# Sums that read a PSUM bank, one bank in the other pool, and moved Sinkhorn steps in a kernel of fifteen-product groups

## The chip, the cores and the metric

The kernel runs on one core of a Trainium2 chip. The metric is the device time of one execution in microseconds (us). Engines are named as in the profile: PE (TensorE; PEld are its weight loads), DVE (VectorE), ACT (ScalarE), POOL (GpSimd), SP (the queue that issues the DMAs).

## The reference

Three parts follow each other: attention of pooled queries, a feed-forward block (here called mish), and a block of eight experts whose outputs are mixed with weights from a Sinkhorn iteration. The change touches the third alone:

```python
def _moe2_ref(x, w_gate, w1, w2):        # x 1152x512, w1 8x512x1024, w2 8x1024x512
    logits = x @ w_gate
    P = np.exp(logits - logits.max())
    for _ in range(8):
        P /= P.sum(1, keepdims=True) + 1e-09
        P /= P.sum(0, keepdims=True) + 1e-09
        P *= N / E
    out = np.zeros((N, D), dtype=np.float32)
    for e in range(E):
        h = np.maximum(x @ w1[e], 0.0)
        out += P[:, e:e + 1] * (h @ w2[e])
    return out
```

## The kernel before, in words

All engines run queues that the program writes in order (a manual schedule); semaphores hold an instruction back until what it reads or overwrites is ready. Attention, the mish block and the first 512 hidden columns of expert 0 come first and aren't touched. Every float32 matmul is made of three matmuls of halves ("h" for the leading bits of a value, "l" for the rest): weights l by data h, h by l, h by h.

**Groups.** The other 60 chunks of 128 hidden columns (4 to 63) are taken in 20 groups of three. A group's hidden layer is a product of a 3x2 block matrix (three chunks, two halves of the 512 inputs) and a 2x3 block matrix (two halves, three stretches of 384 tokens); instead of 18 block products it makes 15, of sums of blocks that were formed beforehand, and then adds and subtracts the products. `ORDER3` is the order of the products: 9, 13, 3, 11, 12, 1, 2, 5, 10, 14, 7, 8, 0, 6, 4. `product` (L973) issues the six matmuls of one, 128x128 by 128x384, into a PSUM bank. `HOME` says which: bank "ft" collects hidden chunk f of the group and token stretch t. Three banks get one product (01, 10, 22); in the other six a second product is added later (00: 13 then 2, 12: 11 then 8, 11: 12 then 5, 02: 10 then 6, 20: 14 then 0, 21: 7 then 4). The first of the two is needed elsewhere, so `after` (L1024) has it read out between the two.

**Pools.** A bank is asked for when its first product is issued (L978). Banks 01, 10 and 22 come from the pool `ps_o` (three banks), the others from `ps_h` (five); the down projection and the matmuls of the Sinkhorn steps use `ps_o` too. A pool hands out the bank that was released longest ago.

**After a product.** `copy` (L1000) has ACT copy a bank into a temporary in SBUF. `pair` (L1004) has DVE add or subtract two temporaries. `fin` (L1013) finishes a block: DVE adds a temporary to the bank in place (L1016), ACT writes the Relu as the leading half `hhall` (L1020), and DVE writes the rest `hlall` (L1021). This last one is put off until the next `fin` has issued its own DVE addition. After each of the first seven products ACT and POOL split the weights of the product eight places later (L74, L81).

**Down projection.** After the products `down` (L1126) takes nine tiles of 128 tokens in the order 0, 1, 2, 6, 7, 8, 3, 4, 5: nine matmuls each, 128x128 by 128x512 (L1145), three for every hidden chunk, and DVE adds the scaled bank to the output (L1153). Between the tiles `next_weights` forms the weight sums of the next group.

**Sinkhorn.** `gate_step` takes the next of ten small steps: the maximum over partitions, its broadcast and the exponential, and eight iterations (`sinkhorn_cols`, L815), each of one small matmul on PE (L817) and a chain of up to six small DVE instructions (L818 to L812), the last of which writes what the next step's matmul reads. The places of the ten steps are written out by hand: in the loop of the last hidden columns of expert 0 (L1108), in the down projection of that part, in the products of groups 0 and 1 (L1197) and in the down projection of group 0 (L1205).

Of the kernel before, what the change touches and what calls it, by code (L numbers as in the profile page):

```python
# [23 lines left out]
def pool_attention_mish_sinkhorn_kernel(  # L24
# [12 lines left out]
    nc = tc.nc  # L37
# [248 lines left out]
    with ExitStack() as actx:  # L286
# [356 lines left out]
        for g in range(T0 + EARLY):  # L643
# [41 lines left out]
            if g == NQ - 1:  # L685
                sctx.close()
                ps_o = ctx.enter_context(tc.tile_pool(name="ps_o", bufs=3, space=PSUM, side="right"))
# [18 lines left out]
    def hidden(c, a, b):  # L706
        return tuple((y if c == NFC - 1 else x[:, c, :])[:, a:b] for x, y in hall)

    ps_h = ctx.enter_context(tc.tile_pool(name="ps_h", bufs=5, space=PSUM))
# [40 lines left out]
    k = EARLY - 1  # L750
# [82 lines left out]
    def expert_up(i, th, c):  # L833
        nonlocal tick
        ps = ps_h.tile([P, 512], F32, tag="h", name=f"ph{i}_{th}_{c}")
        gemm1(ps, i, c, th, x2h, x2l)
        relu_split(hidden(c, th * TH, (th + 1) * TH), ps[:, 0:TH])
        tick += 1
        run_all(tick)
# [35 lines left out]
    def xblock(x, d, t):  # L875
        return x[:, d * HD:(d + 1) * HD, t * TH:(t + 1) * TH]
# [4 lines left out]
    PLUS = {"+": ALU.add, "-": ALU.subtract}  # L881
# [3 lines left out]
    def x_prep(k):  # L885
        n, a, op, b = XSUM[k]
        get = lambda z: xblock(acc, *z) if isinstance(z, tuple) else xsum[z]
        x = xsum[n] = xt_p.tile([P, HD, TH], F32, tag="xt", name=f"xt{n}")
        nc.vector.tensor_tensor(out=x, in0=get(a), in1=get(b), op=PLUS[op])
        x_flush()  # L890
        if k < len(XSUM) - 2:
            Xb[n] = tuple(tsum.tile([P, HD, TH], F32R, name=f"x{n}{y}") for y in "hl")
            x_split(k)

    def x_split(k):
        n = XSUM[k][0]
        split_hi(nc.scalar, Xb[n][0], xsum[n])
        x_lo.append((nc.gpsimd if k % 2 else nc.vector, Xb[n][1], xsum[n], Xb[n][0]))

    def x_flush():  # L900
        while x_lo:
            split_lo(*x_lo.pop(0))
# [27 lines left out]
    def down_split(g, j):  # L930

        if "all" not in wdt:
            wdt["all"] = tuple(wpools["d0"].tile([P, 4, GF], F32R, tag="wd" + x, name=f"wdb{x}") for x in "hl")
        wh, wl = wdt[g, j] = tuple(y[:, (CH * g + j) % 4, :] for y in wdt["all"])
        split_hi(nc.gpsimd, wh, raws_d[g][j])
        split_lo(nc.gpsimd, wl, raws_d[g][j], wh)
# [20 lines left out]
    def w_split(g, k):  # L957
        n = ORDER3[k]
        x = w_get(g, PLAIN[n]) if n in PLAIN else ws[g, n]
        at_ = (NP * g + k) % NSL  # L960
        dst = tuple(y[:, at_, :, :] for y in wslots)
        split_hi(nc.scalar, dst[0], x)
        split_lo(nc.gpsimd, dst[1], x, dst[0])
        Wb[g, n] = dst
# [7 lines left out]
    cb, tmp = {}, {}  # L972
    los = []  # L973

    def product(g, n):
        c = HOME[n]
        if FIRST[n]:
            pl, tag = (ps_o, "o") if c in ("01", "10", "22") else (ps_h, "h")  # L978
            cb[c] = pl.tile([P, 512], F32, tag=tag, name=f"c{c}_{g}")[:, 0:TH]
        (wh, wl), (xh_, xl_) = Wb[g, n], Xb[n]  # L980
        ops = []
        for d in range(HD):
            ops += [(wl[:, d, :], xh_[:, d, :]), (wh[:, d, :], xl_[:, d, :]), (wh[:, d, :], xh_[:, d, :])]
        for m, (a_, b_) in enumerate(ops):
            nc.tensor.matmul(  # L985
                cb[c], lhsT=a_, rhs=b_, start=FIRST[n] and m == 0, stop=LAST[n] and m == len(ops) - 1,
                skip_group_check=True)
# [5 lines left out]
    def temp(g, x):  # L993
        if x in SPARE:
            i = SPARE.index(x)
            tmp[x] = spare[i % 2][:, i // 2, :]
        else:
            tmp[x] = up_t.tile([P, TH], F32, tag=x, name=f"{x}_{g}")

    def copy(g, x, c):  # L1000
        temp(g, x)
        nc.scalar.activation(tmp[x], cb[c], AF.Copy)  # L1002

    def pair(g, eng, out, a, op, b):  # L1004
        if out not in tmp or out == "s11":
            temp(g, out)
        eng.tensor_tensor(out=tmp[out], in0=tmp[a], in1=tmp[b], op=PLUS[op])  # L1007

    def flush_lo():
        while los:  # L1010
            los.pop(0)()

    def fin(g, c, op, x):  # L1013

        b = cb[c]
        nc.vector.tensor_tensor(out=b, in0=b, in1=tmp[x], op=PLUS[op])  # L1016
        flush_lo()
        f, t = int(c[0]), int(c[1])
        hi, lo = hidden(f, t * TH, (t + 1) * TH)
        nc.scalar.activation(hi, b, AF.Relu)  # L1020
        los.append(lambda: nc.vector.scalar_tensor_tensor(  # L1021
            out=lo, in0=b, scalar=0.0, in1=hi.bitcast(F32), op0=ALU.max, op1=ALU.subtract))

    def after(g, n):  # L1024

        v = nc.vector
        if n == 9:
            copy(g, "t9", "01")
        if n == 13:
            copy(g, "t13", "00")  # L1030
            fin(g, "01", "+", "t13")
        if n == 3:
            copy(g, "t3", "10")
            pair(g, v, "s11", "t3", "-", "t9")
        if n == 11:
            copy(g, "t11", "12")
            fin(g, "10", "+", "t11")
        if n == 12:
            copy(g, "u12", "11")
            pair(g, v, "u12", "u12", "-", "t11")  # L1040
        if n == 1:
            copy(g, "t1", "22")
            pair(g, v, "t13", "t1", "+", "t13")
        if n == 2:
            fin(g, "00", "+", "u12")
        if n == 5:
            fin(g, "11", "+", "s11")
        if n == 10:
            copy(g, "t10", "02")
            fin(g, "22", "-", "t10")  # L1050
            pair(g, v, "t3", "t3", "-", "t10")
        if n == 14:
            copy(g, "u14", "20")
            pair(g, v, "u14", "t1", "-", "u14")
        if n == 7:
            copy(g, "u7", "21")
            pair(g, v, "u7", "u7", "+", "t9")
        if n == 8:
            fin(g, "12", "+", "u14")
        if n == 0:  # L1060
            fin(g, "20", "+", "t3")
        if n == 6:
            fin(g, "02", "-", "u7")
        if n == 4:
            fin(g, "21", "-", "t13")
            flush_lo()
# [28 lines left out]
    def gate_step():  # L1095
        if gate_steps:
            gate_steps.pop(0)()
# [7 lines left out]
    with tc.tile_pool(name="xt", bufs=3, side="right") as xt_p:  # L1105
        todo_x = list(range(len(XSUM)))
        for j, u in enumerate(ups):
            if j in (2, 4):  # L1108
                gate_step()
            expert_up(NG1, *u)  # L1110
            for _ in range(2 if j % 2 else 1):
                if todo_x:
                    x_prep(todo_x.pop(0))
        assert not todo_x
        for n, d, t in ((9, 0, 1), (10, 1, 2), (11, 0, 0), (13, 1, 1)):
            Xb[n] = tuple(xblock(x, d, t) for x in (x2h, x2l))
        for k, d, t in ((-2, 0, 2), (-1, 1, 0)):
            Xb[XSUM[k][0]] = tuple(xblock(x, d, t) for x in (x2h, x2l))
            x_split(len(XSUM) + k)
        x_flush()  # L1120
# [56 lines left out]
    def scale(k):  # L1177
        nc.gpsimd.tensor_scalar(
            oacc[:, TILES[k], :], oacc[:, TILES[k], :], Pm[:, TILES[k], 0:1], 0.0, op0=ALU.mult, op1=ALU.add)
# [9 lines left out]
    for g in range(NG):  # L1189
        for k, n in enumerate(ORDER3):  # L1190
            product(g, n)
            after(g, n)
            if k + NSL < NP:
                w_split(g, k + NSL)
            if k in ((0, 7, 9) if g == 0 else (7, 9)):
                down_split(g, {0: 0, 7: 1, 9: 2}[k])
            if k == 9 and g + 1 < NG:  # L1197
                raw_up(g + 1)
            if (g, k) in ((0, 3), (0, 5), (1, 3)):
                gate_step()  # L1200
            if g == 1 and k in (10, 12, 14):
                assert not gate_steps
                scale(k // 2 - 5)
        for k, t in enumerate(TILES):
            down(g, t)  # L1205
            next_weights(g + 1, k)
            if g == 0 and k in (1, 3, 5):
                gate_step()
            if g == 1 and k + 3 < NTT:
                scale(k + 3)  # L1210
# [30 lines left out]
```

## Time and profile before

| | us |
|---|---|
| median of 3 runs | 1261.66 |
| lowest, highest | 1261.29, 1261.70 |
| profiled execution | 1261.36 |
| its span, first to last instruction | 1259.6 |

The profile is that of one execution. Times in it count from the span's start. The page gives the busy time of every engine; the views asked of the trace give groups of instructions by line with their mean duration, waits with what ended them, the chain that ended last (each step followed back to what released it), and the timeline of one engine. Names like `c` are banks of products, `po` banks of the down projection, `t`, `spareh` and `sparel` the temporaries (u12, t10 and u7 lie in `spareh`, t1, u14 and s11 in `sparel`). A matmul's row is longer than the step from one matmul to the next. The granted TensorE clock was 1.0 of full speed in the whole span.

### The profile page before, as it was taken

To read this page: it belongs to the slowest core of one execution; us is meant where nothing else is said; L and a number is where in the kernel's file an instruction comes from. 1 tells how busy PE (TensorE), PEld (TensorE's weight loads), DVE (VectorE), ACT (ScalarE), POOL (GpSimd) and SP (SyncE) were. 2 spreads that over 40 slices of the span, in tenths; PEclk is the share of its full clock that TensorE was granted. 3 is DMA by queue.
4 is the path that set the end of the run, shared out by engine and by line. 5 is a ranking of instruction groups with operands and counts; after the bars stand their busy time and mean duration, and the time that the engine had idled before them with its cause. 6 is when DMAs were issued, how large, how long until landed. Compare 5 with 4: busy or idle time off the path is not lost.

```text
span 1259.6 us, 19402 instructions
## 1 busy us (share of the span) xinstructions
PE 1230.0 (98%) x6832; PEld 1120.1 (89%) x6832; DVE 921.0 (73%) x1706; ACT 622.0 (49%) x1432; POOL 727.3 (58%) x758
## 2 busy tenths in 40 slices
PE   8999999999999999999999999999999999999998
PEld 7999999999999999878888888888888888888887
DVE  7899999975444335797866779877867778866875
ACT  7899999876554433534333333443333334433331
POOL 7888888644434332556656555655555566556552
PEclk9999999999999999999999999999999999999999
DMA  3333333213222110011110111111101111111111
GB/s 114 97 97 91 89 94 96 76 35 118 84 84 85 52 41 17 9 43 50 51 51 28 37 45 48 46 50 51 51 22 39 51 51 42 52 51 39 33 38 75
DMA packets 55760, 73.15 MB, mean 58 GB/s; under 512 B 5744, under 2 KB 37872, under 8 KB 55664
## 3 DMA queue, kind: packets, MB, share of 16 engines
q1 hardware_dynamic: 55664, 71.93, 19.6%
q8 instruction: 54, 0.88, 0.3%
q14 instruction: 42, 0.34, 0.1%
HBM read 64.50 MB, written 2.36 MB: 53 GB/s over the span
## 4 chain that ended last, share of the span: by engine, by line
PE 31%; DVE 13%; issue 6%; ACT 5%
PE po L1145 27%; DVE c L1016 6%; PE c L985 4%; DVE hlall L1021 3%; DVE t L1007 2%; DVE sparel L1007 2%; ACT hhall L1020 1%; ACT t L1002 1%; ACT spareh L1002 1%; ACT wslotsh L74 1%; DVE s L951 0%; DVE spareh L1007 0%; DVE oacc L1151 0%; DVE Pm L810 0%; DVE Pm L819 0%
## 5 line engine op out<-in xcount | busy, mean ns | idle before, releaser
L81 POOL TENSOR_TENSOR wslotsl<-s,wslotsh 128x256 fp32r<-128x256 f32 x180 | 143.4, 806 | 221.2 <-ACT wslotsh L74 221.1
L1153 DVE SCALAR_TENSOR_TENSOR oacc<-po,Pm,oacc 128x512 f32<-128x512 f32 (+1 forms) x217 | 160.7, 744 | 83.8 <-PE po L1145 79.2
L1145 PE MATMUL po<-wdbh,hlall 128*128 128x512 f32 (+1 forms) x543 | 216.2, 398 | 5.7 <-DVE hlall L1021 5.7
L1145 PE MATMUL po<-wdbl,hhall 128*128 128x512 f32 (+1 forms) x543 | 215.7, 397 | 2.9 <-ACT hhall L1020 0.8
L1145 PE MATMUL po<-wdbh,hhall 128*128 128x512 f32 (+1 forms) x543 | 214.0, 394 | 0.0
L1020 ACT ACTIVATE hhall<-c 128x384 fp32r<-128x384 f32 x180 | 88.5, 492 | 161.1 <-DVE c L1016 158.6
L1002 ACT ACTIVATE t<-c 128x384 f32<-128x384 f32 x80 | 39.1, 489 | 224.8 <-PE c L985 224.8
L81 POOL TENSOR_TENSOR wslotsl<-rawu,wslotsh 128x256 fp32r<-128x256 f32 x120 | 97.0, 822 | 68.6 <-ACT wslotsh L74 68.6
L1145 PEld LDWEIGHTS po<-wdbh,hlall 128*128 128x128 f32 x543 | 102.0, 188 | 34.5 <-DVE hlall L1021 12.0
L1145 PEld LDWEIGHTS po<-wdbl,hhall 128*128 128x128 f32 x543 | 102.0, 188 | 33.4 <-issue 10.5
L1145 PEld LDWEIGHTS po<-wdbh,hhall 128*128 128x128 f32 x543 | 102.0, 188 | 23.4
L501 DVE TENSOR_TENSOR etl<-psT,eth 128x384 fp32r<-128x384 f32 (+1 forms) x240 | 112.1, 504 | 9.4 <-ACT eth L498 9.3
L466 POOL TENSOR_SCALAR e<-e,rc 128x1152 f32<-128x1152 f32 x72 | 89.0, 1236 | 43.7 <-DVE rc L465 16.7
L446 DVE TENSOR_SCALAR_CACHE_REDUCE sc<-psS 128x1152 f32<-128x1152 f32 x72 | 97.4, 1353 | 14.5 <-PE psS L441 13.5
L1021 DVE SCALAR_TENSOR_TENSOR hlall<-c,hhall 128x384 fp32r<-128x384 f32 x180 | 97.8, 543 | 2.0
L498 ACT ACTIVATE eth<-psT 128x384 fp32r<-128x384 f32 (+1 forms) x240 | 92.7, 483 | 8.9 <-PE psT L495 8.8
L985 PE MATMUL c<-x2h,wslotsl 128*128 128x384 f32 x280 | 94.4, 337 | 0.0
L985 PE MATMUL c<-x2h,wslotsh 128*128 128x384 f32 x280 | 94.3, 337 | 0.0
L985 PE MATMUL c<-x2l,wslotsh 128*128 128x384 f32 x280 | 94.0, 336 | 0.0
L454 ACT ACTIVATE e<-sc,nm 128x1152 f32<-128x1152 f32 x72 | 92.1, 1279 | 0.5 <-DVE sc L446 0.5
L495 PE MATMUL psT<-ident,e 128*128 128x128 f32 x648 | 85.5, 275 | 1.3 <-POOL e L466 0.8
L166 POOL TENSOR_TENSOR wt<-wt,raw 128x512 int32<-128x512 int32 x32 | 42.1, 1317 | 75.6 <-DVE wt L160 71.0
(349 smaller groups left out, 3302.2 us busy)
## 6 DMA issues: line engine op xcount, KB each, us to landing
rawd<-in_moe_w_dram SPq DMA_DIRECT2D x60, 256.0 KB, 2.6
rawu<-in_moe_w_dram SPq DMA_DIRECT2D x30, 384.0 KB, 3.2
raw<-in_moe_w_in_dram SPq DMA_DIRECT2D x16, 512.0 KB, 3.9
raw<-in_moe_w_out_dram SPq DMA_DIRECT2D x16, 512.0 KB, 3.6
kraw<-in_k_dram SPq DMA_DIRECT2D x16, 288.0 KB, 3.1
vraw<-in_v_dram SPq DMA_DIRECT2D x16, 288.0 KB, 2.8
qraw<-in_q_dram SPq DMA_DIRECT2D x7, 576.0 KB, 4.3
qT<-qT SPq DMA_DIRECT2D x28, 128.0 KB, 2.5
```

The lines of the kernel that those rows point to most:

```text
L81: eng.tensor_tensor(out=lo, in0=src, in1=hi.bitcast(F32), op=ALU.subtract)
L446: nc.vector.tensor_scalar(sc, ps[:, :, 0:TH], -1.0, None, op0=ALU.mult, op1=ALU.min, accum_out=nm)
L454: nc.scalar.activation(e, sc.rearrange("p a b -> p (a b)"), AF.Exp, bias=nm, scale=-1.0, accum_out=rs)
L466: nc.gpsimd.tensor_scalar(e, e, rc, 0.0, op0=ALU.mult, op1=ALU.add)
L495: nc.tensor.transpose(ps[:, i, :], e[:, c * P:(c + 1) * P], ident)
L498: nc.scalar.activation(eh[:, cs, o:o + b - a], ps[:, 0:3, a:b], AF.Copy)
L501: nc.vector.tensor_tensor(out=el[:, cs, o:o + b - a], in0=ps[:, 0:3, a:b], in1=eh[:, cs, o:o + b - a].bitcast(F32), op=ALU.subtract)
L985: nc.tensor.matmul(cb[c], lhsT=a_, rhs=b_, start=FIRST[n] and m == 0, stop=LAST[n] and m == len(ops) - 1, skip_group_check=True)
L1020: nc.scalar.activation(hi, b, AF.Relu)
L1021: los.append(lambda: nc.vector.scalar_tensor_tensor(out=lo, in0=b, scalar=0.0, in1=hi.bitcast(F32), op0=ALU.max, op1=ALU.subtract))
L1145: nc.tensor.matmul(ps[:, 0:w], lhsT=a, rhs=b[:, cs], start=(n == 0), stop=(n == len(ops) - 1))
L1153: nc.vector.scalar_tensor_tensor(out=oa, in0=ps[:, 0:w], scalar=gate, in1=oa, op0=ALU.mult, op1=ALU.add)
```

## The change

Six calls of `pair` now read one operand from the bank itself (written "@", with the block's name). The copies of u12, u14 and u7 on ACT are gone; those of t3, t1 and t10 stay, since the temporaries are read again later. All six sums stay on DVE, and the sum into t3 now stands ahead of the final addition of block 22 instead of behind its two DVE instructions. Bank 21 is asked from `ps_o`. The ten Sinkhorn steps are the same ones, at other places.

```diff
--- before.py
+++ after.py
@@ -975,7 +975,7 @@
     def product(g, n):
         c = HOME[n]
         if FIRST[n]:
-            pl, tag = (ps_o, "o") if c in ("01", "10", "22") else (ps_h, "h")
+            pl, tag = (ps_o, "o") if c in ("01", "10", "22", "21") else (ps_h, "h")
             cb[c] = pl.tile([P, 512], F32, tag=tag, name=f"c{c}_{g}")[:, 0:TH]
         (wh, wl), (xh_, xl_) = Wb[g, n], Xb[n]
         ops = []
@@ -1001,10 +1001,12 @@
         temp(g, x)
         nc.scalar.activation(tmp[x], cb[c], AF.Copy)
 
-    def pair(g, eng, out, a, op, b):
-        if out not in tmp or out == "s11":
+    def pair(g, out, a, op, b):
+
+        a, b = (cb[x[1:]] if x[0] == "@" else tmp[x] for x in (a, b))
+        if out not in ("t13", "t3"):
             temp(g, out)
-        eng.tensor_tensor(out=tmp[out], in0=tmp[a], in1=tmp[b], op=PLUS[op])
+        nc.vector.tensor_tensor(out=tmp[out], in0=a, in1=b, op=PLUS[op])
 
     def flush_lo():
         while los:
@@ -1023,7 +1025,6 @@
 
     def after(g, n):
 
-        v = nc.vector
         if n == 9:
             copy(g, "t9", "01")
         if n == 13:
@@ -1031,30 +1032,27 @@
             fin(g, "01", "+", "t13")
         if n == 3:
             copy(g, "t3", "10")
-            pair(g, v, "s11", "t3", "-", "t9")
+            pair(g, "s11", "@10", "-", "t9")
         if n == 11:
             copy(g, "t11", "12")
             fin(g, "10", "+", "t11")
         if n == 12:
-            copy(g, "u12", "11")
-            pair(g, v, "u12", "u12", "-", "t11")
+            pair(g, "u12", "@11", "-", "t11")
         if n == 1:
             copy(g, "t1", "22")
-            pair(g, v, "t13", "t1", "+", "t13")
+            pair(g, "t13", "@22", "+", "t13")
         if n == 2:
             fin(g, "00", "+", "u12")
         if n == 5:
             fin(g, "11", "+", "s11")
         if n == 10:
             copy(g, "t10", "02")
+            pair(g, "t3", "t3", "-", "@02")
             fin(g, "22", "-", "t10")
-            pair(g, v, "t3", "t3", "-", "t10")
         if n == 14:
-            copy(g, "u14", "20")
-            pair(g, v, "u14", "t1", "-", "u14")
+            pair(g, "u14", "t1", "-", "@20")
         if n == 7:
-            copy(g, "u7", "21")
-            pair(g, v, "u7", "u7", "+", "t9")
+            pair(g, "u7", "@21", "+", "t9")
         if n == 8:
             fin(g, "12", "+", "u14")
         if n == 0:
@@ -1105,7 +1103,7 @@
     with tc.tile_pool(name="xt", bufs=3, side="right") as xt_p:
         todo_x = list(range(len(XSUM)))
         for j, u in enumerate(ups):
-            if j in (2, 4):
+            if j in (2, 5):
                 gate_step()
             expert_up(NG1, *u)
             for _ in range(2 if j % 2 else 1):
@@ -1196,7 +1194,7 @@
                 down_split(g, {0: 0, 7: 1, 9: 2}[k])
             if k == 9 and g + 1 < NG:
                 raw_up(g + 1)
-            if (g, k) in ((0, 3), (0, 5), (1, 3)):
+            if (g, k) in ((0, 3), (1, 0), (1, 4)):
                 gate_step()
             if g == 1 and k in (10, 12, 14):
                 assert not gate_steps
@@ -1204,7 +1202,7 @@
         for k, t in enumerate(TILES):
             down(g, t)
             next_weights(g + 1, k)
-            if g == 0 and k in (1, 3, 5):
+            if g == 0 and k in (1, 4, 7):
                 gate_step()
             if g == 1 and k + 3 < NTT:
                 scale(k + 3)
```

On DVE, twelve rows in the middle of the products of group 10, before (block names follow the c; the last number is a buffer's; the brackets name the engines whose semaphores an instruction waits for, Activation being ACT):

```order
L1021 SCALAR_TENSOR_TENSOR hlall_4458<-c01_10_9926,hhall_4456 128x384
L1007 TENSOR_TENSOR spareh_6717<-spareh_6717,t11_10_9969 128x384 [waits Activation_49]
L1007 TENSOR_TENSOR t13_10_9944<-sparel_6718,t13_10_9944 128x384 [waits DVE_49,Activation_49]
L1016 TENSOR_TENSOR c00_10_9937<-c00_10_9937,spareh_6717 128x384 [waits DVE_49,PE_49]
L1021 SCALAR_TENSOR_TENSOR hlall_4458<-c10_10_9950,hhall_4456 128x384
L1016 TENSOR_TENSOR c11_10_9976<-c11_10_9976,sparel_6718 128x384 [waits PE_49]
L1021 SCALAR_TENSOR_TENSOR hlall_4458<-c00_10_9937,hhall_4456 128x384 [waits Activation_49]
L1016 TENSOR_TENSOR c22_10_9987<-c22_10_9987,spareh_6717 128x384 [waits Activation_49]
L1021 SCALAR_TENSOR_TENSOR hlall_4458<-c11_10_9976,hhall_4456 128x384
L1007 TENSOR_TENSOR t3_10_9957<-t3_10_9957,spareh_6717 128x384
L1007 TENSOR_TENSOR sparel_6718<-sparel_6718 128x384 [waits Activation_49]
L1007 TENSOR_TENSOR spareh_6717<-spareh_6717,t9_10_9933 128x384 [waits Activation_49]
```

and with the change, where a line number is two higher from `fin` on:

```order
L1023 SCALAR_TENSOR_TENSOR hlall_4458<-c01_10_9896,hhall_4456 128x384
L1009 TENSOR_TENSOR spareh_6717<-c11_10_9946,t11_10_9939 128x384 [waits PE_49]
L1009 TENSOR_TENSOR t13_10_9914<-c22_10_9956,t13_10_9914 128x384 [waits DVE_49,Activation_49]
L1018 TENSOR_TENSOR c00_10_9907<-c00_10_9907,spareh_6717 128x384 [waits DVE_49,PE_49]
L1023 SCALAR_TENSOR_TENSOR hlall_4458<-c10_10_9920,hhall_4456 128x384
L1018 TENSOR_TENSOR c11_10_9946<-c11_10_9946,sparel_6718 128x384 [waits PE_49]
L1023 SCALAR_TENSOR_TENSOR hlall_4458<-c00_10_9907,hhall_4456 128x384 [waits Activation_49]
L1009 TENSOR_TENSOR t3_10_9927<-t3_10_9927,c02_10_9989 128x384 [waits Activation_49]
L1018 TENSOR_TENSOR c22_10_9956<-c22_10_9956,spareh_6717 128x384
L1023 SCALAR_TENSOR_TENSOR hlall_4458<-c11_10_9946,hhall_4456 128x384
L1009 TENSOR_TENSOR sparel_6718<-sparel_6718,c20_10_10001 128x384 [waits PE_49]
L1009 TENSOR_TENSOR spareh_6717<-c21_10_10015,t9_10_9903 128x384 [waits PE_49]
```

The sums (L1007, now L1009) read a bank `c` in place of a copy in `spareh` or `sparel`. Those of u12 (from c11), u14 (from c20) and u7 (from c21) now wait for PE alone; those into t13 and t3 still wait for ACT. The sum into t3 moved ahead of the final addition to c22.

On PE, the first matmul of products 5, 14, 7, 0 and 4 of group 10, before:

```order
L985 MATMUL c11_10_9976<-x5h_6399,wslotsl_6533 128x384 [waits Activation_49,Pool_49]
L985 MATMUL c20_10_10032<-x14h_6426,wslotsl_6533 128x384 [waits DVE_49,Pool_49]
L985 MATMUL c21_10_10047<-x7h_6476,wslotsl_6533 128x384 [waits DVE_49,Pool_49]
L985 MATMUL c20_10_10032<-x2h_6011,wslotsl_6533 128x384 [waits Activation_49,Pool_49]
L985 MATMUL c21_10_10047<-x4h_6482,wslotsl_6533 128x384 [waits Activation_49,Pool_49]
```

and with the change:

```order
L985 MATMUL c11_10_9946<-x5h_6399,wslotsl_6533 128x384 [waits DVE_49,Pool_49]
L985 MATMUL c20_10_10001<-x14h_6426,wslotsl_6533 128x384 [waits Pool_49]
L985 MATMUL c21_10_10015<-x7h_6476,wslotsl_6533 128x384 [waits Pool_49]
L985 MATMUL c20_10_10001<-x2h_6011,wslotsl_6533 128x384 [waits DVE_49,Pool_49]
L985 MATMUL c21_10_10015<-x4h_6482,wslotsl_6533 128x384 [waits DVE_49,Pool_49]
```

Products 5, 0 and 4 add to a bank whose first content ACT had read and DVE reads now. Products 14 and 7 start new banks; neither waits for DVE any more.

## Rows read from the trace of the kernel before

**Rows 1.** The page: busy us, share of the span, instructions of PE.

```profile
PE 1230.0 (98%) x6832; PEld 1120.1 (89%) x6832; DVE 921.0 (73%) x1706; ACT 622.0 (49%) x1432; POOL 727.3 (58%) x758
```

**Rows 2.** Waits of PE: us in total, times, longest us.

```profile
PE c L985 <- DVE hlall L1021: 6.2, 19, 0.3
PE po L1145 <- DVE hlall L1021: 5.7, 19, 0.3
```

**Rows 3.** Chain that ended last, group 10: start us, us, what.

```profile
894.89 2.10 PE c L985 x12
...
904.18 0.46 DVE hlall L1021
...
913.50 17.53 PE po L1145 x74
...
931.04 2.10 PE c L985 x12
```

**Rows 4.** Timeline of PE in group 10: start us, us, instruction, idle before it.

```profile
905.03 0.34 PE L985 MATMUL c<-x14h,wslotsh 128*128 128x384 f32 x1
905.72 0.42 PE L985 MATMUL c<-x7h,wslotsl 128*128 128x384 f32 x1 [0.34 <-DVE hlall L1021]
905.97 0.34 PE L985 MATMUL c<-x7l,wslotsh 128*128 128x384 f32 x1
906.15 0.34 PE L985 MATMUL c<-x7h,wslotsh 128*128 128x384 f32 x1
...
912.21 0.40 PE L1145 MATMUL po<-wdbh,hhall 128*128 128x512 f32 x1
912.73 0.47 PE L1145 MATMUL po<-wdbl,hhall 128*128 128x512 f32 x1
913.50 0.50 PE L1145 MATMUL po<-wdbh,hlall 128*128 128x512 f32 x1 [0.30 <-DVE hlall L1021]
913.84 0.40 PE L1145 MATMUL po<-wdbh,hhall 128*128 128x512 f32 x1
```

**Rows 5.** DVE's groups of L1007: busy us, mean ns, idle us before them.

```profile
L1007 DVE TENSOR_TENSOR spareh<-spareh,t 128x384 f32<-128x384 f32 x40 | 49.3, 1232 | 14.6 <-ACT spareh L1002 14.6
L1007 DVE TENSOR_TENSOR t<-t,spareh 128x384 f32<-128x384 f32 x20 | 24.2, 1210 | 0.0
L1007 DVE TENSOR_TENSOR t<-sparel,t 128x384 f32<-128x384 f32 x20 | 20.8, 1041 | 0.4 <-ACT sparel L1002 0.4
L1007 DVE TENSOR_TENSOR sparel<-sparel 128x384 f32<-128x384 f32 x20 | 19.2, 960 | 0.0
L1007 DVE TENSOR_TENSOR sparel<-t,t 128x384 f32<-128x384 f32 x20 | 16.1, 806 | 24.8 <-ACT t L1002 24.8
```

**Rows 6.** The low halves, L1021: ns min/median/max, first and last start.

```profile
L1021 DVE SCALAR_TENSOR_TENSOR hlall<-c,hhall x180: 537/541/559, 534.8 to 1239.9; 128x384 fp32r<-128x384 f32 x180
```

**Rows 7.** The final additions, L1016: columns as in rows 6.

```profile
L1016 DVE TENSOR_TENSOR c<-c,t x80: 546/550/567, 531.8 to 1238.8; 128x384 f32<-128x384 f32 x80
```

**Rows 8.** Timeline of ACT in group 10: columns as in rows 4.

```profile
898.13 0.49 ACT L1020 ACTIVATE hhall<-c 128x384 fp32r<-128x384 f32 x1 [0.63 <-DVE c L1016]
898.52 0.41 ACT L74 ACTIVATE wslotsh<-s 128x256 fp32r<-128x256 f32 x1
898.83 0.48 ACT L1002 ACTIVATE t<-c 128x384 f32<-128x384 f32 x1
...
899.50 0.49 ACT L1002 ACTIVATE t<-c 128x384 f32<-128x384 f32 x1
```

**Rows 9.** Timeline of PE at Sinkhorn steps and group 0's product 7.

```profile
494.65 0.38 PE L802 MATMUL psb<-m,ones 1*128 1x1 f32 x2 [0.40 <-DVE m L798]
...
537.00 0.39 PE L817 MATMUL psk<-csum,ones 128*128 128x8 f32 x2 [0.23 <-DVE csum L812]
...
541.91 0.41 PE L985 MATMUL c<-x7h,wslotsl 128*128 128x384 f32 x1 [0.22 <-DVE hlall L1021]
...
557.90 0.39 PE L817 MATMUL psk<-csum,ones 128*128 128x8 f32 x2 [0.95 <-DVE csum L812]
```

## The prediction, made before the result was known

> **What bounds the kernel now.** I read four views in this order. The page first: PE is busy for 98% of the span [rows 1], so only a change that lets matmuls start earlier can help. Then the list of waits: PE waits for DVE's `hlall` 19 times ahead of a product (L985) and 19 times ahead of a down tile (L1145) [rows 2], once per group in 19 of the 20 groups, so this is a pattern of the group and not an accident. Then the chain that ended last, in group 10: from PE's first two products at 894.89 it runs through DVE and ACT alone and comes back to PE only at 913.50; the next group starts at 931.04, 36.15 us after this one [rows 3]. PE is busy all that time, but the group's end is timed by DVE's and ACT's queue. Last, PE's own timeline of that group shows what this costs [rows 4]. Matmuls of 384 columns start 0.175 us apart. Between 905.03 and 906.15, at product 7, three steps take 1.12 in place of 0.52 us: 0.60 lost. Matmuls of 512 columns start 0.233 us apart. Between 912.21 and 913.84, in the first down tile, three steps take 1.63 in place of 0.70: 0.93 lost. That is 1.53 us a group, and without them a group would take 34.62. (The idle times of these rows, 0.34 and 0.30, say less: a matmul's row is 0.34 to 0.50 long and overlaps the next, so I count from start to start.)
>
> Product 7 waits because its bank "21" is the sixth that a group asks of a pool of five: it gets the bank of "00" once `hlall` of that block is written. The first down tile waits for `hhall` and `hlall` of block "20". Both come late because DVE executes its queue in order, with six sums of temporaries (L1007) in it.
>
> **Part 1: six sums read a bank.** Now the operands of all six lie in SBUF, and the sums take 0.81 to 1.23 us [rows 5]; weighted by their counts the six take 129.6 us over 120, 1.08 each. After the change each has one operand in PSUM, one in SBUF, and writes to SBUF. No row has just this sum; the nearest is L1021, which reads and writes from and to the same memories at the same size: 0.541, between 0.537 and 0.559 over 180 executions [rows 6]. L1016, which reads and writes the bank, lies between 0.546 and 0.567 [rows 7]. Neither varies with what GpSimd does, while the sums of today do. I take X = 0.54. The ends: 0.54 (nothing of this size with a bank is quicker) and 1.23 (the dearest group of today's sums). DVE loses 6 x (1.08 - 0.54) = 3.2 us of work a group, ACT three copies.
>
> [...]
>
> Does the shorter queue clear both stalls? I follow it in group 10 with X open. A copy on ACT blocks its queue for 0.39 us after a Relu starts and for 0.31 after a weight split starts [rows 8]; on DVE the next instruction starts 0.46 after the last one [rows 3]. The copy of t11 ends at 899.99 [rows 8] as now. Final sum "10" (0.02 + 0.55) ends at 900.56, its Relu and two weight splits hold ACT until 901.59, and the copy of t1 ends at 902.08; today the copy of u12 stands before it. The order keeps the sum into t13 waiting for this copy, as the two read one bank. It starts at 902.10. Then in order: final sum "00" at 902.02 + X, low half of "10" 0.47 later, final sum "11" from 902.95 + X to 903.50 + X, its Relu on ACT, behind it the copy of t10, ended at 904.40 + X; the sum into t3 (which waits for that copy), final sum "22", low half of "11", and the sum u14, which ends at 905.27 + 3X. With X = 0.54 this is 906.89.
>
> **The new waits.** Three products now add into a bank that DVE, not ACT, has to have read: 5 after u12, 0 after u14, 4 after u7. u12 follows the low half of "01" and ends at 901.47; product 5 starts 18 steps of 0.175 before product 7's due start of 905.2, at 902.0: no wait. Product 0 starts ten steps after 906.15 [rows 4], at 907.90; without the 0.60 at product 7 that is 907.30, and its first weights load one step before, at 907.13. u14 is done 0.24 ahead of that, which is the tightest place of the change (it bears X up to 0.62). What queues behind u14 on DVE are u7 and the final sums of 12, 20, 02, 21; each of these from "12" on then waits for PE. Product 6 ends its matmuls six steps after product 0, at about 909.6; final sum "02" takes until 910.1, the low half of "20" behind it until 910.6. The first down tile asks for it two steps after its matmul of 912.21, less 0.60, at 912.1. The 0.93 are gone with over 1 us to spare.
>
> **Part 2: bank "21" moves to the pool of three.** It takes the bank of "01", whose low half is written at about 901.0, four us before product 7. The 0.60 are gone. The third down tile now gets the bank of "21" instead of "22"; it starts 4.2 us after the products end, and low half "21" ends about 2 us after them. No wait. Without this part product 7 would still wait for `hlall` of "00", but that would be earlier too.
>
> **Part 3: Sinkhorn steps at other products.** One matmul each; the work is the same. Steps that stood too close made PE idle for 0.40 (the broadcast of the maximum), 0.23 and 0.95 us [rows 9]; each is now put further from the one before it. The two in group 1 come closer to theirs (a tile and a product, 3.1 us). I count 1.58 gained less 0.5 for a new wait there: 1.1, with ends 0 and 1.6.
>
> **Sum.** 18 groups x 1.53 = 27.5. Group 0 waits 0.22 at product 7 where the others wait 0.34 [rows 4, 9]: 1.4. Of the 20 groups 19 wait [rows 2]; group 1 has nothing to gain. Part 3: 1.1. Together 30.0 us. The profiled execution took 1261.36, so 1231.4; the median of the runs is 0.3 above it, so **1231.7 us**. I expect no new bound from GpSimd: at both places PE's waits name DVE and not the weight splits [rows 2].
>
> **Rivals.**
> - *The margin of 0.24 us is not there* (chance 0.13). Above X = 0.62 product 0 waits for u14, three times the excess, as three sums stand in its chain. For it: two of the six take the bank as second operand, which no row shows. Against: L1021's spread of 0.02. At X = 0.80 the group loses 3 x 0.18 = 0.54, in 18 groups 10 us: 1241.
> - *The bank wait moves instead of going* (0.05). If the pool of three hands bank "21" a block that is still read, 0.60 stays in 18 groups, 10.8 us: 1242.5. Against it speak the four us above.
> - *Reading a bank costs as much as today's sums or more* (0.05): slower. Then the 1.2 us of ACT's copies saved are given back on PE, because PE now waits for sums on DVE at products 5 and 0 where it waited for short copies. The loss at product 0 is 3 x (X - 0.62), plus X - 0.76 since final sum "10" then waits for s11 (it could start at 899.25 + X, later than 900.01). From X = 1.04 on this exceeds the 1.53 of today. At 1.23 it is 1.83 + 0.47 = 2.30, so 0.77 x 18 = 13.9 more, less 1.1 of part 3: 1274.5. For it: every L1007 row was dearer than 0.8. [...] Against it: the narrow spread of what reads a bank today [rows 6, 7].
> - *The chain stays as long* (0.02): X near 1.04, no change within 2.5 us.
>
> **How the numbers follow.** My forecast has a chance of 0.75 and its own range, 1229.5 to 1233.5, from part 3's ends and X between 0.54 and 0.62 in a few groups. The range for 8 in 10 reaches from 1229 up into the first rival and to the edge of the second, 1242; beyond it lie about 0.15. Runs of this kernel can tell a difference of 0.2% (2.5 us). Faster: 0.75 + 0.13 + 0.05 = 0.93; the same 0.02; slower 0.05.
>
> **What would show it.** Right: the six sums at 0.54 to 0.57 us each with no spread; no PE idle before product 7's `x7h` and in the first down tile; groups 34.6 us apart; ACT with 60 copies fewer; in the chain of waits PE takes the place of DVE and ACT. The first rival: an idle PE of 0.1 to 0.6 us ahead of product 0 (`x2h` behind `x7h` and product 8), ended by a DVE sum into `sparel`. The second: PE idle ahead of `x7h` as now. The third: sums above 1 us, and idle PE at products 5 and 0. I am wrong outside 1229 to 1242, and also if the time is right with stalls left at either place.

## The result, and the profile after

The changed kernel takes **1230.72 us** (median of 4 runs, 1230.40 to 1231.02); the kernel before took 1261.49 on the same chip (4 runs, 1261.29 to 1261.70). The ratio is 0.9756, 95% interval 0.9739 to 0.9773: faster by 30.8 us, where 1231.7 was predicted. The profiled execution took 1231.02 us, 1229.2 of it the span, at the same clock of 1.0.

The page of the changed kernel, its row of engines, which answers to [rows 1]:

```profile
PE 1215.2 (99%) x6832; PEld 1124.4 (91%) x6832; DVE 864.0 (70%) x1706; ACT 599.6 (49%) x1372; POOL 694.6 (57%) x758
```

The same 6832 matmuls; ACT has 60 instructions fewer (the copies); DVE has as many as before and 57 us less work. GpSimd's time fell too, by 33 us with the same 758 instructions. The sums come first, as L1009 where [rows 5] had L1007 (ns min/median/max, then first and last start):

```profile
L1009 DVE TENSOR_TENSOR spareh<-c,t x40: 547/550/553, 537.5 to 1203.5; 128x384 f32<-128x384 f32 x40
L1009 DVE TENSOR_TENSOR sparel<-c,t x20: 558/558/558, 534.2 to 1195.9; 128x384 f32<-128x384 f32 x20
L1009 DVE TENSOR_TENSOR t<-c,t x20: 547/557/558, 537.9 to 1198.7; 128x384 f32<-128x384 f32 x20
L1009 DVE TENSOR_TENSOR t<-t,c x20: 554/554/556, 541.1 to 1201.6; 128x384 f32<-128x384 f32 x20
L1009 DVE TENSOR_TENSOR sparel<-sparel,c x20: 543/546/547, 542.5 to 1203.0; 128x384 f32<-128x384 f32 x20
```

All 120 lie between 543 and 558 ns, whichever operand is the bank. PE's waits in the expert block, to be set beside [rows 2] (us in total, times, longest us):

```profile
PE c L985 <- DVE hlall L1023: 1.1, 1, 1.1
PE psk L817 <- DVE csum L812: 1.0, 1, 1.0
PE c L985 <- DVE crec L818: 0.9, 1, 0.9
```

Both waits that came 19 times are gone. What is left comes once each, at a Sinkhorn step or just behind one. The chain that ended last, in a stretch around group 10 as in [rows 3] (start us, us, what):

```profile
860.84 18.90 PE po L1143 x81
879.73 15.74 PE c L985 x90
895.47 18.90 PE po L1143 x81
914.37 15.74 PE c L985 x90
```

No DVE or ACT piece is left in it. A group is 90 matmuls of products and 81 of the down projection without a gap, 15.74 + 18.90 = 34.64 us; [rows 3] had 36.15. PE's timeline at product 7 and at product 0 of that group, against [rows 4]:

```profile
889.89 0.34 PE L985 MATMUL c<-x14h,wslotsh 128*128 128x384 f32 x1
890.06 0.34 PE L985 MATMUL c<-x7h,wslotsl 128*128 128x384 f32 x1
890.24 0.34 PE L985 MATMUL c<-x7l,wslotsh 128*128 128x384 f32 x1
890.41 0.34 PE L985 MATMUL c<-x7h,wslotsh 128*128 128x384 f32 x1
...
891.99 0.34 PE L985 MATMUL c<-x2h,wslotsh 128*128 128x384 f32 x1
892.17 0.33 PE L985 MATMUL c<-x2h,wslotsl 128*128 128x384 f32 x1
892.35 0.33 PE L985 MATMUL c<-x2l,wslotsh 128*128 128x384 f32 x1
```

From one start to the next it is 0.17 to 0.19 us everywhere. The last two rows are the start of product 0, the one that must not start before the sum u14 is done. That sum, on DVE:

```profile
891.32 0.55 DVE L1009 TENSOR_TENSOR sparel<-sparel,c 128x384 f32<-128x384 f32 x1
```

It ends at 891.87; the product's first weights load one step before 892.17, at 892.00. The margin is 0.13 us.

**Where the time came from**, by the starts of the groups on PE in the two traces:

| stretch | before | after | difference |
|---|---|---|---|
| start to group 0 | 528.9 | 529.5 | +0.6 |
| group 0 | 40.4 | 36.7 | -3.7 |
| group 1 | 36.2 | 36.3 | +0.2 |
| groups 2 to 18, each | 36.15 | 34.63 | -1.52 (17 times: -25.9) |
| group 19 to the end | 39.48 | 37.94 | -1.54 |

Together -30.4, the difference of the two spans. Group 0's 3.7 are its own two stalls (0.46 at product 7, 0.97 in the first down tile), two waits at Sinkhorn steps (0.50 and 1.59) and a step that stands in group 1 now (0.2).

### The profile page after: what moved, and what is told of

It reads as the page before. It is cut to its first block, busy times and chain, and to the rows that moved or that the text cites. A ratio compares the mean times of both kernels' runs of the same rounds, so it can differ in the third digit from the quotient of the medians.

```text
span 1229.2 us, 19310 instructions
## 1 busy us (share of the span) xinstructions
PE 1215.2 (99%) x6832; PEld 1124.4 (91%) x6832; DVE 864.0 (70%) x1706; ACT 599.6 (49%) x1372; POOL 694.6 (57%) x758
## 4 chain that ended last, share of the span: by engine, by line
PE 92%; DVE 4%; ACT 1%; issue 1%; POOL 1%; POOLq 0%; ACTq 0%; DVEq 0%
PE po L1143 31%; PE c L985 25%; PE ph L219 9%; PE po L725 8%; PE psS L441 7%; PE psA L520 6%; PE psT L495 5%; DVE sc L446 1%; DVE xt L889 1%; PE psk L379 1%; PE psq L421 0%; PE pg L780 0%; PE psw L581 0%; DVE hlall L830 0%; POOL wslotsl L81 0%
## 5 line engine op out<-in xcount | busy, mean ns | idle before, releaser
L81 POOL TENSOR_TENSOR wslotsl<-s,wslotsh 128x256 fp32r<-128x256 f32 x180 | 131.9, 741 | 239.9 <-ACT wslotsh L74 239.9
L81 POOL TENSOR_TENSOR wslotsl<-rawu,wslotsh 128x256 fp32r<-128x256 f32 x120 | 90.6, 769 | 51.9 <-ACT wslotsh L74 51.9
```

Source lines behind the costliest of these rows:

```text
L81: eng.tensor_tensor(out=lo, in0=src, in1=hi.bitcast(F32), op=ALU.subtract)
```

## The experiments

Each was timed beside the kernel before on its own chip (medians 1261.34 to 1261.87).

**Each part alone.** The first has part 1 of the diff (`pair` and its six calls) and nothing else.

> The six sums read a bank, bank 21 stays in the pool of five and the Sinkhorn steps stay where they were. One-queue theory (both stalls of a group come from DVE's late queue): all of the gain of the groups, 34.6 us a group and no PE idle at product 7, since the low half of 00 is then written at about 904.5 in the clock of group 10 of before, 0.5 us ahead of need; 1230 to 1233 us. Rival, two causes (the wait at product 7 is one for a sixth bank, the wait in the down tile one for DVE's sums): 0.5 to 0.6 us at product 7 stay in 18 groups, about 1241 us.

Measured: **1231.4 us** (1231.15 to 1231.61), ratio 0.9759 [0.9744, 0.9773]. PE has no wait for `hlall` at a product or a down tile any more, and groups are 34.63 us apart. The second has part 2 alone:

```diff
-            pl, tag = (ps_o, "o") if c in ("01", "10", "22") else (ps_h, "h")
+            pl, tag = (ps_o, "o") if c in ("01", "10", "22", "21") else (ps_h, "h")
```

> Only bank 21 moves to the pool of three. One-queue theory: PE goes through product 7 without a wait and loses the same 0.6 us at the next places that want DVE (product 0, first down tile); a group still takes 36.1 us, 1261 us within 2. Rival, two causes: 0.6 us less in 18 groups, about 1251 us.

Measured: **1261.63 us**, ratio 0.9998 [0.9989, 1.0008]. This is the most instructive of the runs: the wait at product 7 is indeed gone, and the time is the same. PE's waits:

```profile
PE po L1145 <- DVE hlall L1021: 5.7, 19, 0.3
PE po L1145 <- ACT hhall L1020: 5.4, 19, 0.3
PE c L985 <- ACT sparel L1002: 3.2, 18, 0.2
```

and PE's timeline in group 10, at product 0 and at the first down tile:

```profile
907.73 0.34 PE L985 MATMUL c<-x2h,wslotsh 128*128 128x384 f32 x1
908.25 0.42 PE L985 MATMUL c<-x2h,wslotsl 128*128 128x384 f32 x1 [0.18 <-ACT sparel L1002]
908.51 0.34 PE L985 MATMUL c<-x2l,wslotsh 128*128 128x384 f32 x1
...
912.65 0.40 PE L1145 MATMUL po<-wdbh,hhall 128*128 128x512 f32 x1
913.33 0.47 PE L1145 MATMUL po<-wdbl,hhall 128*128 128x512 f32 x1 [0.28 <-ACT hhall L1020]
914.10 0.50 PE L1145 MATMUL po<-wdbh,hlall 128*128 128x512 f32 x1 [0.30 <-DVE hlall L1021]
914.44 0.40 PE L1145 MATMUL po<-wdbh,hhall 128*128 128x512 f32 x1
```

Product 0 now loses 0.78 - 2 x 0.175 = 0.43 us, and the first down tile 1.79 - 3 x 0.233 = 1.09 in place of 0.93. The 1.52 of the group (0.43 + 1.09) are all still there, 0.43 of them at a new place, and groups are still 36.16 apart: PE reaches the queue of DVE and ACT earlier and waits for the same end of it. The third has part 3 alone:

```diff
-            if j in (2, 4):
+            if j in (2, 5):
...
-            if (g, k) in ((0, 3), (0, 5), (1, 3)):
+            if (g, k) in ((0, 3), (1, 0), (1, 4)):
...
-            if g == 0 and k in (1, 3, 5):
+            if g == 0 and k in (1, 4, 7):
```

> Only the ten Sinkhorn steps move. All theories: within 2 us of the kernel before, 1259.5 to 1262.5. Its trace shows which of PE's waits at steps go and come: if the later exponential delays DVE, a wait of about 1 us stands after the eighth tile ahead of group 0 here as well.

Measured: **1259.83 us**, ratio 0.9984 [0.9974, 0.9993]: 2.0 us faster. The fourth is the whole change without part 3 (those three lines as they were before):

> Both changes of the groups, Sinkhorn steps where they were before. If the new places are worth the 1.1 us that the prediction counted: 1231.8 us. If the wait of 1.1 us that the changed kernel shows at the step after the eighth tile ahead of group 0 comes from the later exponential, that wait is absent here and 0.5 us stands at the broadcast of the maximum instead; the steps in group 0 then decide. The traces tell these apart, the times hardly.

Measured: **1231.58 us** (1231.47 to 1233.17), ratio 0.9763 [0.9749, 0.9778]. So on top of parts 1 and 2, part 3 brings some 0.9 us by the medians, which come from two chips, and 0.5 when each is taken from the kernel before on its own chip (30.3 and 30.8 us gained). Part 2 brings nothing (1231.4 without it and part 3, 1231.58 with it).

**What makes part 1 work: cheaper sums, or fewer copies?** This run has the whole change, but ACT still copies the three banks into the temporaries, as before, and each of the three sums then writes over the copy, for which it has to wait:

```diff
+            copy(g, "u12", "11")
             pair(g, "u12", "@11", "-", "t11")
...
+            copy(g, "u14", "20")
             pair(g, "u14", "t1", "-", "@20")
...
+            copy(g, "u7", "21")
             pair(g, "u7", "@21", "+", "t9")
```

> The changed kernel, with ACT's copies of u12, u14 and u7 back in their places; nothing reads them, and each sum waits for the copy of its bank as before. Theory that DVE's shorter sums are all of it: as the changed kernel, 1231 us. Theory that the copies stand on the path too (t1's copy waits behind that of u12, and the sum of u12 behind its own): product 5 waits for u12 about 0.5 us and product 0 for u14 about 0.3, so a group takes 35.3 to 35.4 us and the whole about 1244.

Measured: **1247.48 us** (1247.27 to 1247.62), ratio 0.9886 [0.9870, 0.9903]. The sums stay at 553 to 557 ns in the mean by group, yet groups are 35.53 us apart. The chain that ended last has ACT in it again (start us, us, what):

```profile
893.63 0.30 ACT wslotsh L74
893.93 0.39 ACT spareh L1002
894.32 0.02 issue
894.35 0.57 DVE spareh L1009
894.91 0.14 issue
895.05 5.49 PE c L985 x30
```

The copy of u12 queues behind a Relu and a weight split on ACT, the sum u12 waits for it, and product 5 loses 0.58 us; product 0 loses another 0.31. So the sums that read a bank bring 0.62 of the 1.52 us a group while the copies stay, and the other 0.90 need the copies gone. The next run asks why the old sums were dear. It is the kernel before, in which GpSimd splits the down weights of a group's second and third chunk only for group 0; the down projection of the later groups multiplies by older weights there. Copies and sums are those of before:

```diff
     def down_split(g, j):
+        if g > 0 and j > 0:
+            return
```

> The kernel before, with GpSimd's splits of the second and third chunk's down weights left out from group 1 on (those chunks use stale weights). These splits run beside DVE's sums t3, u14 and u7. Theory that GpSimd's work beside them makes these sums dear: they fall from 1.22, 0.96 and 1.65 to about 0.55 us, the wait in the first down tile goes, the one at product 7 (ahead of these splits) stays: 35.1 to 35.2 us a group, about 1243. Rival (two operands in SBUF cost that by themselves): sums and time as before, 1261.

Measured: **1244.82 us** (1244.37 to 1244.92), ratio 0.9865 [0.9850, 0.9880], groups 35.24 apart. Its sums (L1009 in this kernel), ns min/median/max:

```profile
L1009 DVE TENSOR_TENSOR spareh<-spareh,t x40: 550/810/1652, 536.5 to 1217.4; 128x384 f32<-128x384 f32 x40
L1009 DVE TENSOR_TENSOR sparel<-t,t x20: 633/818/824, 533.3 to 1208.7; 128x384 f32<-128x384 f32 x20
L1009 DVE TENSOR_TENSOR t<-sparel,t x20: 547/1092/1094, 537.2 to 1212.0; 128x384 f32<-128x384 f32 x20
L1009 DVE TENSOR_TENSOR t<-t,spareh x20: 546/549/1215, 542.8 to 1216.3; 128x384 f32<-128x384 f32 x20
L1009 DVE TENSOR_TENSOR sparel<-sparel x20: 559/559/960, 544.0 to 1216.9; 128x384 f32<-128x384 f32 x20
```

Two groups of sums that stood beside the splits fell from 1210 and 960 in the mean [rows 5] to 549 and 559 in the median (584 and 596 in the mean), and the mixed first group from 1232 to 723 in the mean. The two groups that stand beside the weight splits of the products, which still run, kept their price (818 and 1092; 806 and 1041 in the mean before). Of the 120 sums 54 have no GpSimd instruction beside them in this run, and these take 546 to 560 ns each; in the group that starts its products near 887 us, the three beside weight splits take 0.82, 0.82 and 1.09 us, and t3, u14 and u7, while GpSimd is idle, 0.55, 0.56 and 0.55. So what was dear was not a sum of two SBUF operands by itself but one beside GpSimd's work. This run, in which the copies stay, gets 0.92 of the 1.52 us a group; the wait at product 7 stays (6.1 us in 19 times), where the chain that ends there still runs through ACT's copies and the sums that stayed dear.

**How much the margin bears.** Two runs turn one sum each back to SBUF operands. The first is that into t3, ahead of u14 in DVE's queue; it reads the copy of t10, which is there anyway:

```diff
-            pair(g, "t3", "t3", "-", "@02")
+            pair(g, "t3", "t3", "-", "t10")
```

> The changed kernel, but the sum into t3 reads the copy t10 in SBUF instead of the bank; its place in the queue stays. It stands ahead of u14, for which product 0 has a margin of 0.2 us by the prediction's working. With its duration X3 in the trace, product 0 should wait X3 - 0.76 us in every group: at 0.8 to 1.2 us that is 0.05 to 0.45, so 1231.5 to 1239 us. If the margin is larger than worked out: no wait, 1230.7.

Measured: **1233.19 us** (1232.91 to 1233.26), ratio 0.9773 [0.9759, 0.9788]. The sum and PE at product 0:

```profile
L1009 DVE TENSOR_TENSOR t<-t,spareh x20: 577/774/777, 540.9 to 1203.7; 128x384 f32<-128x384 f32 x20
```

```profile
892.91 0.34 PE L985 MATMUL c<-x2h,wslotsh 128*128 128x384 f32 x1
893.14 0.41 PE L985 MATMUL c<-x2h,wslotsl 128*128 128x384 f32 x1
893.39 0.34 PE L985 MATMUL c<-x2l,wslotsh 128*128 128x384 f32 x1
```

The sum is 0.22 us longer than with the bank (0.774 against 0.554, at the same place in the queue), and product 0 loses 0.48 - 0.35 = 0.13; groups are 34.77 apart, 0.13 more. The first rival's place and mechanism are real, then: the changed kernel has about 0.1 us left there. What was expected, a wait of this sum's time less 0.76, would have been 0.01: the margin set in there was too large. The second run does the same to u7, with its copy, behind u14 in the queue:

> The changed kernel, but u7 is copied by ACT and summed from SBUF as before (1.6 us then). It stands behind u14, where the working leaves 0.6 us at product 4 and over 0.8 us at the first down tile: no wait, 1230.7 within 1. If any DVE work in the products is paid for, 1.1 us in 20 groups: about 1250.

Measured: **1231.28 us** (1231.00 to 1231.38), ratio 0.9758 [0.9744, 0.9773]; this sum takes 0.773 in the median, and groups stay 34.63 apart. The same extra work behind the tight place costs nothing in the groups.

**The Sinkhorn steps.** Two of the remaining waits stand at product 1, in groups 0 and 1, shortly after a step. A step's matmul takes one of the three banks of `ps_o`, from which the first products want three as well. This run moves the steps in the groups away from there, behind the fifteenth product of group 0 and the eighth of group 1, and puts the exponential back to place 4 in the loop of expert 0's last hidden columns:

```diff
-            if j in (2, 5):
+            if j in (2, 4):
...
-            if (g, k) in ((0, 3), (1, 0), (1, 4)):
+            if (g, k) in ((0, 14), (1, 7)):
...
-            if g == 0 and k in (1, 4, 7):
+            if g == 0 and k in (1, 3, 5, 7):
```

> Both changes of the groups, with the Sinkhorn steps at third places: the broadcast of the maximum one product earlier than in the changed kernel, then after the last product of group 0, after its tiles 2, 4, 6 and 8, and after product 5 of group 1, so that no step asks a bank of the pool of three between the requests for 01 and 22. If PE's waits of about 1.1 us at product 1 of groups 0 and 1 come from the step's bank, and the one after the eighth tile from the later exponential, all three go and 0.65 us come back at the broadcast: 2.5 to 3 us less than the changed kernel, about 1228. If the steps, two tiles apart, wait for each other as in the kernel before: 1 us of that is lost again.

Measured: **1229.76 us** (1229.58 to 1229.92), ratio 0.9750 [0.9737, 0.9763]; the changed kernel, run once more on that chip:

> The changed kernel itself on the same chip, to compare with: 1230.7 us within 0.5.

Measured: 1230.69 (1230.27 to 1231.32), 0.9 more, where a gain of 2.5 to 3 us, or 1 us less than that, was expected. The waits at product 1 and the one ahead of group 0 are gone, so the steps ahead of product 1 were the cause there; but two others, of steps too close behind the one before, are there, at the broadcast of the maximum and in the down projection of group 0:

```profile
494.60 0.38 PE L802 MATMUL psb<-m,ones 1*128 1x1 f32 x2 [0.40 <-DVE m L798]
...
554.65 0.39 PE L817 MATMUL psk<-csum,ones 128*128 128x8 f32 x2 [0.62 <-DVE csum L812]
```

The last version spreads these too, with the run before it repeated on the same chip:

```diff
-            if j in (2, 4):
+            if j in (1, 4):
...
-            if g == 0 and k in (1, 3, 5, 7):
+            if g == 0 and k in (2, 4, 6, 8):
```

> The steps of the Sinkhorn work placed as in the run with cleared steps, but the two of an up tile at products 1 and 4 instead of 2 and 4, and those of the first down tile at products 2, 4, 6, 8 instead of 1, 3, 5, 7. If each step waits only for the vector work of the step ahead of it and a wider gap covers that, the waits of the run with cleared steps ahead of group 0 (some 0.8 us) and the psb wait (some 0.6 us) go: about 1228.4 us. If the vector work of two neighbouring steps is longer than any gap of two or three products, the waits only move: 1229 to 1229.8 us. The groups' step stays 34.63 us by both.

> The run with cleared steps once more, on the chip of the run with spread steps, so that the two can be set side by side: 1229.8 us, as there.

Measured: **1228.5 us** (1227.78 to 1228.64), ratio 0.9737 [0.9724, 0.9751], against 1229.26 (1229.04 to 1229.94). The same two steps:

```profile
494.39 0.38 PE L802 MATMUL psb<-m,ones 1*128 1x1 f32 x2
...
555.41 0.28 PE L817 MATMUL psk<-csum,ones 128*128 128x8 f32 x2
```

No step waits any more in this trace; it is that of the fastest of the four executions, 0.7 us ahead of the other three. This version is the fastest of the study: by the two comparisons on one chip each, 0.9 and 0.8 us, it is 1.7 below the changed kernel, by the medians across chips 2.2; what remains is the groups' 34.63, in which PE has no gap.

## Why the prediction was right, step by step

**The bound and the 1.53 us a group: right.** Start to start, 0.60 and 0.93 us were lost; the groups became 1.52 shorter. The 27.5 us for 18 groups stand against 25.9 + 1.5 = 27.4 in the table. That it is one queue of DVE and ACT that times a group's end, not two separate stalls, is what two runs show: with part 2 alone one stall is removed and nothing gained, with part 1 alone both go.

**X = 0.54 for a sum that reads the bank: right**, 0.543 to 0.558 in all 120, and so the third and fourth rivals fell. The reason given, that L1021 is the nearest row because it neither varies nor depends on GpSimd, holds: in the trace before, 60 of its 180 executions have no GpSimd instruction beside them and take 0.537 to 0.557 us, and 44 have one for over 80% of their time and take 0.540 to 0.548. Nor were the sums of two SBUF operands dear by themselves: in the run without GpSimd's splits of the second and third chunk two groups of them take 0.549 and 0.559 us in the median, as much as the sums with a bank.

**The margin at product 0: there, but half the size.** I worked out 0.24 us and the trace has 0.13. Counted from the group's start, u14 ends at 12.14 (891.87 - 879.73), worked out were 12.00 (906.89 - 894.89). Some 0.04 of the 0.14 are three sums and additions at 0.55 to 0.56 where 0.54 was set; the final addition into "10" (its row: 884.90, 0.57 long) ends at 5.74, worked out were 5.67 (900.56), and the rest is gaps of that size between the engines. It didn't decide, but 0.22 us more ahead of it cost time.

**Part 2: right that there is no wait, and it does nothing in this kernel.** I wrote that without it product 7 would still wait for `hlall` of "00", only for an earlier end; with part 1 alone there is no such wait, as that block is written early enough.

**Part 3: the 1.1 came out by luck; its terms are wrong.** I summed idle times (0.40 + 0.23 + 0.95), though I had said of [rows 4] that only start to start counts. Start to start, against a step that does not wait, the three lost 0.46, 0.50 and 1.59: 2.5 us. The largest of them I put down to part 3, but it is part 1 that removes it: with the sums alone and the steps at their old places, PE's waits at these steps come down from 1.2 us in two waits to

```profile
PE psk L817 <- DVE csum L812: 0.2, 1, 0.2
```

On the other side I counted 0.5 for a new wait; there are two. The wait at product 1 of group 1 is 1.26, where before it was 1.05. And a step that I counted as free now loses 1.21, ahead of group 0:

```profile
529.29 0.36 PE L817 MATMUL psk<-csum,ones 128*128 128x8 f32 x2 [0.97 <-DVE csum L812]
```

The exponential went one place later in the loop of expert 0's last hidden columns, and DVE, which waits in its queue for ACT's `Pm`, waits longer: in the changed kernel

```profile
507.63 0.24 DVE L808 TENSOR_REDUCE rsum<-Pm 128x9 f32<-128x81 f32 x1 [2.51 <-ACT Pm L804]
```

and in the kernel before

```profile
504.18 0.24 DVE L808 TENSOR_REDUCE rsum<-Pm 128x9 f32<-128x81 f32 x1 [1.51 <-ACT Pm L804]
```

so all that queues behind it comes later. With the exponential back at place 4 this wait is gone, in the run without part 3 and in the one with cleared steps. How long it is changes between executions: the changed kernel's second trace, from another chip, has 0.36 in place of 0.97, and four other runs with the steps at these places have 0.38. The difference is one small vector instruction ahead of this step, with two SBUF operands. It took 0.23 us in the second trace and 0.83 in the first:

```profile
527.98 0.83 DVE L810 TENSOR_TENSOR Pm<-Pm,rsum 128x72 f32<-128x72 f32 x1
```

GpSimd works beside it in both traces, so why it was longer in one is not shown. In the first trace the net is 2.5 - 1.21 - 0.21 = 1.1, and 1.59 of the 2.5 are part 1's. Part 3 gains 2.0 us alone and 0.5 to 0.9 on top of the rest. "Group 1 has nothing to gain" was true of this placing alone: a wait at product 1 hides what the other groups lose; with the step moved away, the group takes 34.8.

**The first and second rival** did not come about; the first lay 0.13 us away. With the steps at their old places the first does come about in one group: in group 0 of the run without part 3, product 0 starts 0.47 late behind u14.

## What to carry to other kernels

Before two waits are summed, ask whether they stand in one queue: removing the first may only move its time to the next, and the run that removes one alone shows it at no gain (here the 0.60 us of product 7 came back as 0.43 at product 0 and 0.16 in the first down tile, and groups stayed 36.16 us apart). In this kernel a sum of temporaries that reads one operand from the bank did two things at once: it dropped the copy ahead of it, and beside GpSimd's work it took 0.54 to 0.56 us, where the sums of two SBUF operands took 0.55 to 1.65. It took both: 0.62 of 1.52 us a group came with cheap sums and the copies kept, 0.92 with the copies kept and three of the six sums made cheap by a quieter GpSimd. No run has the copies gone and the sums still dear, so the shares of the two are not told apart further. Count stalls from start to start everywhere, in the small terms too, and place small steps where they compete neither for a bank nor with the vector work of the step before (worth 0.9 and 0.8 us here, each compared on one chip).

## What was not expected of the hardware

A sum with both operands in SBUF took 0.55 to 0.56 us with GpSimd quiet and up to 1.65 beside it, with the same instruction, size and memories; with one operand in PSUM it took 0.54 to 0.56 in all 120 cases, though GpSimd worked beside 99 of them for over 60% of their time. GpSimd gained as well, 727.3 to 694.6 us with as many instructions. That the dear sums follow GpSimd's work is shown by the 549 against 1210 ns above; what ties the two together, no run shows.
